# Sigmoid attention with a gated convolution: fewer groups in plain float32, and a new written-out order

## The chip, the cores and the metric

The kernel runs on one core of a Trainium2 chip. The metric is the device time of one execution in microseconds (us). The kernel before was run three times, with times of 561.61, 561.38 and 561.16 us (median 561.38).

## The reference

`q`, `k` and `v` have 8 batches, 12 heads, 448 positions and 64 columns per head, in float32. Cut to what matters, the reference computes:

```python
scores = q @ k.T / sqrt(64) - log(448)      # per batch and head
attn   = sigmoid(scores)                    # elementwise, no row sum
x      = heads_side_by_side(attn @ v)       # [8, 448, 768]
gate   = sigmoid(causal_conv(x, conv_w))    # 5 taps, per column
val    = x @ w_val                          # [768, 768]
out    = (gate * val) @ w_out               # [768, 768]
```

## The kernel before, in words

**Work units.** The 96 heads are 48 pairs (two heads lie on the 128 partitions), and two pairs are a group, so there are 24 groups. Three groups make one batch position block b of 448 + 64 columns on which the convolution and the two products by `w_val` and `w_out` run.

**Scores.** A pair's scores are three chunks of a PSUM tile `ps_a` (three buffers, taken in turn). If the pair is in `WHOLE_SCORES`, the operands are `qk_single` as loaded, in float32, and TensorE makes one pass in plain float32 (L575). Otherwise `split_qk` first makes `qk_hi` (a cast, L395 or L391) and `qk_lo` (a subtraction on GpSimd, L404), and TensorE makes three passes on these. In the trace, one plain float32 matmul is two instructions.

**Attention.** If a group is in `WHOLE`, ScalarE writes the sigmoid of a tile into `a_single` (L611), and TensorE multiplies that by `v_src` as loaded (L661 for the 64 positions left over, L669 for the chunks). Otherwise there is more to do for the group. VectorE takes the largest value of each row of `v_src` (`vm`, L590); TensorE sums it over partitions with a small matmul (L595) that shares the tile and the step with the left-over scores (L598), so these scores wait for `vm`; VectorE makes the exponent `v_exp` from the sum (L603, L632, L634, L636); `v_src` is split in `v_hi` and `v_lo`; and each sigmoid tile is written in place into `ps_a` (L611), scaled to float16 by ScalarE (L399) and its remainder taken by VectorE (L622).

**After the attention.** The result is copied out of `ps_a` into `x` (L391, L395, or L399 with a scale). VectorE takes `x_max` (L717). A small matmul with `diagonal` (L761) spreads the largest value of a block, and `x` is split into `xs` (L804). The five taps of the convolution make `gate`: a first scaling, then for each tap either a multiply-and-add by VectorE (L738), or a scaling into `tap` and a DMA that adds `tap` to `gate` (L742, a gate sum). L744 is the gate's sigmoid.

**Weights.** Twelve blocks of `w_val` and `w_out` come as 64-bit words. `convert` and `weight` turn each into float32 with five steps (L425, L427, L401 or L399, L450, and the largest value, L453). For each two blocks TensorE sums the largest values over partitions (L463), VectorE makes the scales (L435, L437, L439), and the blocks are split into `w_hi` and `w_lo` (L401 or L399, then L490).

**What sets the order.** Nothing is scheduled on the chip or in the build: every operation gets a number when the program is laid out, and the table `ORDER` (two characters for an operation) says in what order they are issued, `ENGINES` (one letter each) on which engine each runs. Within an engine the instructions run in that order, and loads stand in it too, on SyncE's queue (SP). GpSimd's instructions take turns with VectorE's on a shared port. `v_src` has two buffers, so the load of a group waits until the attention two groups before it has ended.

Of the kernel before, what the change touches and what calls it, by code (L numbers as in the profile page):

```python
# [37 lines left out]
WHOLE = {0, 1, 2, 3, 4, 5, 6, 7}  # L38
WHOLE_SCORES = {0, 1, 2, 3, 4, 5, 6, 7, 8, 9, 10, 11, 12, 13, 14, 15}
# [70 lines left out]
    "0d3x4009423D4443453E4s3F3G3H3J4t3K4u4y484d3L0b494v463M4w4a4O4b3W4x4C4c4A0c4D4F4E4e4G4f4I0g4H4B4J4g0e1c4L1d4K4h"  # L110
    "4M574i584P4j5d594k4l4Q4N4m4q4o5a5b4R4p4n4U5c5h5f5i5k4r5j5l4S5w5n5m5Y5o0j5q5g5p0h5r4V0f5R6J4W0k5S4T5T5X4X5s4Y5U"
    "5x5V5y4Z5W5z4+5+7u7v6e5Z6K4-500i51606f536h52556g6i546k6j5A6l5C6n96976m5t610m6o676C6862566D6p6E5-6q6I0n636F646G"
    "5B656H5D6-3I5E6L70726N5F715G7375745H76786677796O5I696r7n5J5K5L6s7o5P7p5u5N7a5O6P7q6a6Q6w7t0l7r6R9U6b6M7s7M6S7w"
    "6c5v7N5Q7P7O7x7Q7S0p7R6x0o7T7b7y7V6t7U7Y6u7W8-6U7Z90be6V6y7+95916vbf7X7-80929V6z81826A93836T7z94846W7A9p0r987B"
    "9q856X7C9r6d868i1e8999878j8a9s7D8b6Y9t888k9u8l6Z7E9b8c7c7F8m6B7G8d9cca8e7d7H8n8fbg9v8g9w9y5M9z9x9A9a9E9C8o8r1g"
    "0q9G8s9D9H8A7I8B9d7h1faX8t9F7Je98C7ebh8u9f7f7K8D6+9J8E1h9g8Fbi8p8vbj9I9e8w9Kbk8x8G9M8y0s9h9L1i7i9N9R7g1k9S9Obl"
    "abbm9P1jacbn9i9T7L1l9Qbo9jag0u9W8hbpfmahaj0tai7jam8J1mak8z8K9l8L9Z9X9m8H8S7k8Tal8Man9k9Bad8q8U1nbq8Nap9Y7l8Oaq"
    "8V7mbrae8Waoea8X1o9+asaraY8Iat8Pauav8Y1pcfaJ8Qcg9naDawaxco8RaG1qchaf8ZciaEcp9-cja1ayaMbscqa28+craHfna0csazaFct"
# [1146 lines left out]
```

## Time and profile before

| | before |
|---|---|
| median of three runs (561.16 to 561.61) | 561.38 us |
| span of the profiled execution | 559.5 us |
| TensorE (PE) busy | 554.8 us (99%) |
| VectorE (DVE) busy | 487.4 us (87%) |
| ScalarE (ACT) busy | 429.7 us (77%) |
| GpSimd (POOL) busy | 200.8 us (36%) |

The span goes from the first instruction to the end of the last one in one profiled execution; the time of a run is some 1.9 us longer, by the median and the span. A busy TensorE isn't a TensorE at its peak, since the ends of matmuls are modelled; how long TensorE takes for a piece of work is read here from the start of one group of matmuls to the start of the next.

### The profile page before, as it was taken

Reading aid. Unit: us, or ns where it says so; the run is one execution under the profiler, and the core shown is the slowest. Engines: PE = TensorE matmul, PEld = TensorE weight load, DVE = VectorE, ACT = ScalarE, POOL = GpSimd, SP = SyncE. Lnnn points to the kernel's source line nnn. Section 1 sums busy time; section 2 is a strip of 40 time slices with the busy share of each in tenths; the row PEclk is TensorE's granted clock in tenths of the full one; section 3 lists DMA queues with packets and bytes.
Section 4 is the critical chain, followed back from the end, with each engine's and each line's share of the span. In section 5 each row is a group of like instructions: output and inputs, shape, how many; then the busy total and the mean of one; then the engine's idle time right before and its main releaser. Section 6 shows DMA issues by size and latency. Waiting matters only on the chain.

```text
span 559.5 us, 10606 instructions
## 1 busy us (share of the span) xinstructions
PE 554.8 (99%) x4061; PEld 325.1 (58%) x4061; DVE 487.4 (87%) x844; ACT 429.7 (77%) x572; POOL 200.8 (36%) x211
## 2 busy tenths in 40 slices
PE   9999999999999999999999999999999999999997
PEld 4343334455554567855466754678555874456686
DVE  1878999999999999998999999998899888896653
ACT  5676687889999989999989878899858978443220
POOL 0000012454345655535364653454523523404100
PEclk9999999999999999999999999999999999999999
DMA  8888687855776537576376685467365657437314
GB/s 294 298 306 282 202 264 145 206 129 130 176 188 148 133 97 199 110 208 136 74 177 169 148 175 147 128 150 190 94 158 127 158 100 169 77 76 134 74 36 154
DMA packets 40371, 89.04 MB, mean 159 GB/s; under 512 B 14976, under 2 KB 21248, under 8 KB 40320
## 3 DMA queue, kind: packets, MB, share of 16 engines
q1 hardware_dynamic: 30272, 55.58, 30.6%
q0 software_dynamic: 8928, 31.99, 30.2%
q10 hardware_dynamic: 1120, 0.79, 0.4%
q8 instruction: 32, 0.52, 0.4%
q14 instruction: 19, 0.16, 0.1%
HBM read 43.96 MB, written 12.40 MB: 101 GB/s over the span
## 4 chain that ended last, share of the span: by engine, by line
PE 99%; ACT 0%; DVE 0%; issue 0%
PE ps_m L1053 34%; PE ps_a L575 19%; PE ps_a L669 17%; PE ps_m L978 15%; PE ps_a L978 7%; PE ps_a L598 4%; PE ps_a L661 3%; PE ps_m L1096 1%; PE ps_m L463 0%; ACT y_mixed L399 0%; PE ps_a L764 0%; DVE ones L1089 0%; PE ps_m L761 0%; PE ps_a L463 0%; PE ps_a L595 0%
## 5 line engine op out<-in xcount | busy, mean ns | idle before, releaser
L1053 PE MATMUL ps_m<-xs,w_val_hi 128*128 128x512 f16 x504 | 150.1, 379 | 0.0
L611 ACT ACTIVATE ps_a<-ps_a 128x896 f32<-128x896 f32 x112 | 99.5, 907 | 16.5 <-PE ps_a L575 9.8
L742 POOL DMA_DIRECT2D gate<-tap x60 | 53.5, 892 | 152.9 <-DVE gate L738 37.3
L622 DVE SCALAR_TENSOR_TENSOR a<-ps_a,a 128x896 f16<-128x896 f32 x96 | 101.9, 1082 | 3.6 <-ACT a L399 3.5
L1053 PE MATMUL ps_m<-xs,w_val_lo 128*128 128x512 f16 x252 | 95.5, 379 | 0.0
L404 POOL TENSOR_TENSOR qk_lo<-qk_src,qk_hi 128x448 fp32r<-128x448 f32 (+1 forms) x64 | 72.2, 1133 | 63.3 <-DVE qk_hi L395 11.5
L399 ACT ACTIVATE a<-ps_a 128x896 f16<-128x896 f32 x96 | 86.7, 921 | 0.6
L1053 PEld LDWEIGHTS <-w_val_hi 128*128 128x128 f16 x504 | 47.8, 98 | 56.0 <-issue 6.4
L978 PEld LDWEIGHTS <-mixed 128*128 128x128 f16 x648 | 62.4, 98 | 13.0 <-issue 3.7
L611 ACT ACTIVATE a_single<-ps_a 128x896 f32<-128x896 f32 x56 | 47.5, 925 | 11.1 <-PE ps_a L575 6.3
L978 PE MATMUL ps_m<-form,mixed 128*128 128x256 f16 x432 | 54.2, 273 | 0.0
L669 PE MATMUL ps_a<-a,v_hi 128*64 128x448 f16 x384 | 52.7, 354 | 0.0
L399 ACT ACTIVATE tap<-x,cw 128x512 f32<-128x512 f32 x62 | 44.4, 729 | 2.2 <-DVE x L720 2.2
L1053 PEld LDWEIGHTS <-w_val_lo 128*128 128x128 f16 x252 | 24.7, 98 | 29.7
L575 PE MATMUL ps_a<-qk_single 64*128 64x448 f32 x192 | 39.6, 558 | 0.0
L575 PE MATMUL ps_a<-qk_hi 64*128 64x448 f32 x192 | 39.5, 407 | 0.0
L669 PE MATMUL ps_a<-a_single,v_src 128*64 128x448 f32 x192 | 37.8, 543 | 0.0
L978 PE MATMUL ps_m<-form,w_out_hi 128*128 128x256 f16 x216 | 37.6, 273 | 0.0
L738 DVE SCALAR_TENSOR_TENSOR gate<-x,cw,gate 128x512 f32<-128x512 f32 x48 | 36.3, 760 | 0.1
L978 PEld LDWEIGHTS <-w_out_hi 128*128 128x128 f16 x324 | 31.2, 98 | 8.6 <-issue 1.8
L575 PE MATMUL ps_a<-qk_lo,qk_hi 64*128 64x448 f32 x192 | 35.4, 362 | 0.0
L575 PE MATMUL ps_a<-qk_hi,qk_lo 64*128 64x448 f32 x192 | 35.3, 361 | 0.0
(176 smaller groups left out, 1063.5 us busy)
## 6 DMA issues: line engine op xcount, KB each, us to landing
gate<-tap POOLq DMA_DIRECT2D x60, 512.0 KB, 5.1
qk_src<-qk SPq DMA_DIRECT2D x32, 448.0 KB, 4.1
v_src<-vs SPq DMA_DIRECT2D x24, 448.0 KB, 4.7
...
qk_single<-qk SPq DMA_DIRECT2D x15, 448.0 KB, 7.2
...
```

The source lines that it names most:

```text
L399: nc.scalar.activation(to, x, AF.Copy, scale=by)
L404: engines[eng].tensor_tensor(to, x, y, op=ALU.subtract)
L575: mm(b()[:, h, :S], k()[rows, at : at + P], q()[rows, :S], start=(n == 0), stop=(n == len(terms(i)) - 1))
L598: mm(b()[to, h, :S], x[n]()[rows, CW:], x[n]()[rows, :S], start=True, stop=True)
L611: nc.scalar.activation(to, b()[:, :, :S], AF.Sigmoid, bias=-math.log(S), scale=1.0 / math.sqrt(D))
L622: op({"V": 1.0}, t + 0.5, lambda e: nc.vector.scalar_tensor_tensor(part(1), p(), A_SCALE, part(0), op0=ALU.mult, op1=ALU.subtract), [b], [ ...
L661: mm(px()[to, p, :S], v()[rows, h * D : (h + 1) * D], x(s["a"])[rows, h, at : at + S], start=(j > 0 and n == 0), stop=(j == 0 and n == len ...
L669: mm(px()[to, p, :S], v()[:, o : o + D], x(st[2 * j + p]["a", c])[:, h, at : at + S], start=(j == 0 and c == 0 and n == 0), stop=(j > 0 an ...
L738: op({"V": 0.67}, at + AT["tap_step"] * k + AT["tap_pair"] * p, lambda e, p=p, part=part, k=k: nc.vector.scalar_tensor_tensor(part(), x()[ ...
L742: op({"G": 0.95}, at + AT["tap_step"] * k, lambda e, tap=tap: nc.gpsimd.dma_start(g(), tap(), accum_op=ALU.add), [tap], [g], 4 * P * T * 4 ...
L978: mm(to(), stat[a](), src()[:, f, :], start=(first and c == 0 and j == 0), stop=(c == NQ - 1 and j == 2), skip_group_check=True)
L1053: mm(po()[:, cs], w()[:, c, :], x(k)[:, cs], start=(c == 0 and j == 0), stop=(c == NC - 1 and j == 2))
```

## The change

Group 7 leaves `WHOLE`, and pairs 12 to 15 leave `WHOLE_SCORES`: their attention and scores are then made as those of the later groups are. `ORDER` and `ENGINES` are replaced as a whole, since the operations and their numbers change.

```diff
-WHOLE = {0, 1, 2, 3, 4, 5, 6, 7}
-WHOLE_SCORES = {0, 1, 2, 3, 4, 5, 6, 7, 8, 9, 10, 11, 12, 13, 14, 15}
+WHOLE = {0, 1, 2, 3, 4, 5, 6}
+WHOLE_SCORES = {0, 1, 2, 3, 4, 5, 6, 7, 8, 9, 10, 11}
...
 ORDER = (
-    "3U004z5e0102030504193s3y3e3f3h3g3i3k3j3l3n3m3o3q3p3N0a3r0608073O473P3t3u3Q1a3v3R3z3S1b3A3V3X3T3B3Y3w3+3Z3C3-41"
...
+    "48003u013v3w023x3A3y3z3D3B043C3E03053F3I3J3K3L3M063O07084n3N3P3Q3R3G0a414243443H0b45464b494c474d3S4e4f4h4i4g4k"
```

The two tables have two more lines in the change, so its line numbers are two higher: L592 in the rows of the change is L590 of before.

The first place is VectorE's beginning: the first two blocks of `w_val` up to the scales. Before:

```order
L425 TENSOR_SCALAR w_words<-w_words 128x768
L427 TENSOR_SCALAR w_words<-w_words 128x768
L425 TENSOR_SCALAR cw_words<-cw_words 128x30
L401 TENSOR_SCALAR w_words<-w_words 128x768
L425 TENSOR_SCALAR w_words<-w_words 128x768
L427 TENSOR_SCALAR cw_words<-cw_words 128x30
L427 TENSOR_SCALAR w_words<-w_words 128x768
L401 TENSOR_SCALAR w_words<-w_words 128x768
L450 SCALAR_TENSOR_TENSOR w_words<-w_words 128x768 x2
L453 TENSOR_REDUCE val_max<-w_words 128x1 x2
```

and in the change:

```order
L427 TENSOR_SCALAR w_words<-w_words 128x768
L429 TENSOR_SCALAR w_words<-w_words 128x768
L403 TENSOR_SCALAR w_words<-w_words 128x768
L452 SCALAR_TENSOR_TENSOR w_words<-w_words 128x768
L455 TENSOR_REDUCE val_max<-w_words 128x1
L427 TENSOR_SCALAR w_words<-w_words 128x768
L429 TENSOR_SCALAR w_words<-w_words 128x768
L403 TENSOR_SCALAR w_words<-w_words 128x768
L452 SCALAR_TENSOR_TENSOR w_words<-w_words 128x768
L455 TENSOR_REDUCE val_max<-w_words 128x1
```

Where steps of two blocks alternated, each block now goes through its five steps one behind the other, each step reading what the one ahead of it wrote. The same holds for the blocks that follow.

The second place is TensorE where the left-over scores of group 7 stand, behind the scores of pairs 12 and 13 (`diagonal` is the spread of the first block's largest value). Before:

```order
L575 MATMUL ps_a<-qk_single 128x448 x12
L598 MATMUL ps_a<-qk_single 64x448 x4
L661 MATMUL ps_a<-a_single,v_src 64x448 x4
L761 LDWEIGHTS ones
L761 MATMUL ps_m_757<-diagonal,ones 128x128
L669 MATMUL ps_a<-a_single,v_src 64x448 x12
L575 MATMUL ps_a<-qk_single 128x448 x6
```

and in the change, from the last chunk of pair 13:

```order
L577 MATMUL ps_a<-qk_hi 128x448 x2
L577 MATMUL ps_a<-qk_hi,qk_lo 128x448 x2
L577 MATMUL ps_a<-qk_lo,qk_hi 128x448 x2
L763 LDWEIGHTS ones
L763 MATMUL ps_m_771<-diagonal,ones 128x128
L597 LDWEIGHTS ones
L597 MATMUL ps_a<-vm,ones 128x1
L600 MATMUL ps_a<-qk_src 64x448 x4
L663 MATMUL ps_a<-a_single,v_src 64x448 x4
L671 MATMUL ps_a<-a_single,v_src 64x448 x12
```

The sum of `vm` now stands ahead of the left-over scores, and the small matmul of `diagonal` has moved ahead of both.

The third place is VectorE just ahead of that `vm`. Before, around the `x_exp` that makes `diagonal`:

```order
L717 TENSOR_REDUCE x_max<-x 128x2
L425 TENSOR_SCALAR w_words<-w_words 128x768
L720 COPY x<-x 128x2x6x4
L401 TENSOR_SCALAR w_words<-w_words 128x768
L755 TENSOR_REDUCE x_exp<-x_max 128x1
L450 SCALAR_TENSOR_TENSOR w_words<-w_words 128x768
L401 TENSOR_SCALAR tap<-x,cw 128x512
```

and in the change:

```order
L452 SCALAR_TENSOR_TENSOR w_words<-w_words 128x768
L455 TENSOR_REDUCE out_max<-w_words 128x1
L505 TENSOR_SCALAR y_scale<-val_inverse,y_inverse 128x6
L397 CAST qk_hi<-qk_src 128x448
L397 CAST qk_hi<-qk_src 128x384
L437 TENSOR_SCALAR out_inverse<-ps_m_728 128x2
L719 TENSOR_REDUCE x_max<-x 128x2
L757 TENSOR_REDUCE x_exp<-x_max 128x1
L592 TENSOR_REDUCE vm<-v_src 128x1
```

Casts of `qk_src` and the `vm` of group 7 stand here now, and the third block of `w_out` is converted ahead of them.

## Rows read from the trace of the kernel before

**Rows 1.** The page: the chain that ended last, share of the span by engine.

```profile
PE 99%; ACT 0%; DVE 0%; issue 0%
```

**Rows 2.** Busy time by engine in two stretches: PE, PEld, DVE, ACT, POOL, clock.

```profile
12.50:420.00 407.50, 407.50 (x2957) 226.86 (x2954) 383.43 (x659) 350.35 (x465) 164.64 (x168) 1.00 0.65 172
145.00:300.00 155.00, 155.00 (x1227) 93.23 (x1227) 149.50 (x258) 148.22 (x199) 80.64 (x81) 1.00 0.59 143
```

**Rows 3.** Timeline of PE, pairs 12 to 14: start, duration, engine, line.

```profile
72.94 4.78 PE L575 MATMUL ps_a<-qk_single 64*128 64x448 f32 x24
77.65 0.98 PE L598 MATMUL ps_a<-qk_single 64*64 64x448 f32 x8
78.45 0.93 PE L661 MATMUL ps_a<-a_single,v_src 64*64 64x448 f32 x8
79.32 0.23 PE L761 MATMUL ps_m<-diagonal,ones 128*128 128x128 bf16 x1
79.48 4.73 PE L669 MATMUL ps_a<-a_single,v_src 128*64 128x448 f32 x24
84.14 2.53 PE L575 MATMUL ps_a<-qk_single 64*128 64x448 f32 x12
86.60 0.60 PE L1053 MATMUL ps_m<-xs,w_val_hi 128*128 128x512 f16 x2
```

**Rows 4.** Timeline of PE, a group whose operands are split.

```profile
155.94 0.17 PE L595 MATMUL ps_a<-vm,ones 128*128 128x1 bf16 x1
156.04 0.98 PE L598 MATMUL ps_a<-qk_src 64*64 64x448 f32 x8
156.84 0.56 PE L661 MATMUL ps_a<-a_rest,v_hi 64*64 64x448 f16 x8
...
161.04 0.47 PE L575 MATMUL ps_a<-qk_hi 64*128 64x448 f32 x2
...
163.09 0.61 PE L1053 MATMUL ps_m<-xs,w_val_hi 128*128 128x512 f16 x2
```

**Rows 5.** Timeline of PE: the first two sums of the weights' largest values.

```profile
21.74 0.25 PE L463 MATMUL ps_m<-val_max,ones 128*128 128x1 bf16 x4
...
34.62 0.25 PE L463 MATMUL ps_m<-val_max,ones 128*128 128x1 bf16 x4
```

**Rows 6.** Timeline of DVE: in brackets the idle time ahead, and its releaser.

```profile
12.52 0.56 DVE L425 TENSOR_SCALAR w_words<-w_words 128x768 int32<-128x768 uint32 x1 [11.51 <-DMA w_words<-w_val]
...
22.03 0.16 DVE L435 TENSOR_SCALAR val_inverse<-ps_m 128x2 int32<-128x2 int32 x1 [1.62 <-PE ps_m L463]
...
42.84 0.56 DVE L425 TENSOR_SCALAR w_words<-w_words 128x768 int32<-128x768 uint32 x1 [0.36 <-DMA w_words<-w_val]
43.43 1.04 DVE L427 TENSOR_SCALAR w_words<-w_words 128x768 int16<-128x768 int16 x1
44.25 0.93 DVE L453 TENSOR_REDUCE val_max<-w_words 128x1 bf16<-128x768 f32 x1
45.09 0.55 DVE L401 TENSOR_SCALAR w_words<-w_words 128x768 f32<-128x768 f32 x1
...
62.78 0.19 DVE L720 COPY x<-x 128x48 f32<-128x48 f32 x1 [0.38 <-ACT x L391]
```

**Rows 7.** DVE's groups by line and shape: count, busy us, mean ns.

```profile
L622 DVE SCALAR_TENSOR_TENSOR a<-ps_a,a 128x896 f16<-128x896 f32 x96 | 101.9, 1082 | 3.6 <-ACT a L399 3.5
L738 DVE SCALAR_TENSOR_TENSOR gate<-x,cw,gate 128x512 f32<-128x512 f32 x48 | 36.3, 760 | 0.1
...
L590 DVE TENSOR_REDUCE vm<-v_src 128x1 bf16<-128x896 f32 x16 | 17.3, 1078 | 0.0
L427 DVE TENSOR_SCALAR w_words<-w_words 128x768 int16<-128x768 int16 x12 | 12.6, 1052 | 0.2
...
```

**Rows 8.** DMA issues: count, KB each, median us from issue to landing.

```profile
v_src<-vs SPq DMA_DIRECT2D x24, 448.0 KB, 4.7
```

**Rows 9.** ACT's largest group of scalings: count, busy us, mean ns.

```profile
L399 ACT ACTIVATE tap<-x,cw 128x512 f32<-128x512 f32 x62 | 44.4, 729 | 2.2 <-DVE x L720 2.2
```

More of the change, by code (lines that the diff above doesn't have):

```diff
@@ L108 @@
 ORDER = (
-    "3U004z5e0102030504193s3y3e3f3h3g3i3k3j3l3n3m3o3q3p3N0a3r0608073O473P3t3u3Q1a3v3R3z3S1b3A3V3X3T3B3Y3w3+3Z3C3-41"
[L110 to L118, printed above, removed]
@@ new lines @@
+    "094l4j4m4I4J3T3U3V3W3X3Z3+4P4K4L4M4N4S3-4O4T4Q4V4U4W4X5u4t404o4p4q0d4r4s4u52194Y4Z4-504+5n5o4v0c4w4x5p5q4y4a4z"
+    "4A5t4B0e5r1a4C4D4E4F4G1b4H5354515s5v5x5y5A5z5B5D5C5G5E5F5H5I65666768696a55564R57585M1c0g0h6c6d595a5b5c5d5e6b6e"
+    "5N5O5f0f6u5g5h6x0j6v5j1d6w6A6y6f6B6z6D6E6C5k6S6T6U6V5w1e6W6g5S5P5l6F6n6X6Y6o6h1g6q6i6j6k0k6Z7K0i1f6-7f7g1h7h7i"
+    "7l7j7m7k7o7n7D7p7E6+5J5m9qat6G6l6m5Q5T6p7q5R71725U5V780l7F7G7H735W74751i3Y1k1j1l5i5K5X707I7J806r6H0m0n796I766J"
+    "0o6s777M7a8182837L6K6L5L5Y1m1o1n8486878589885Z7N8c8d8e9f8a1p9g9i9j7P8b9k9l1q8f5+8g0p7Q8h5-619h9n629J8i636t9m8j"
@@ new lines @@
+    "9o8l7O7b9O9r1s9s8k9p649K9L8m6M9P8n9R9Q0r6N9S8y8z6O8A8p6P8o8q8r8s8t8u8B1u8C1r9U6Q9V9X1tbw1wbP9Y9T1v9M9v7V8D6R7r"
+    "9W8v9Z8EbQ9+7W7c0qaia11xbRau7R9N7S7T7U9-a07d8w8Fa9aca28H9u7s8Q8I8R8S8J8T8U8V8K8Gaaada31y1z9wa5afa7ab1Aae7taga8"
+    "8La68M7X1Baj7e7u7xbSakalaqarahbTbUeK0s8N8O7Yamanaoapas8Wav8XbVaRaSaTaM8P7ZaN7v7w0ufX8Z8+96aO97987y7z7A7BaXaU7+"
+    "a+bW9zaVaYa-bX999a7CaW1C1DaZbY8Yb07-8x8-9b90919293b1b2b4bZ1E9cb3b51Fb+60a494bc0tbd9dbl9e959xbe9yaP9C9A9BbfaQcQ"
+    "cRcLbicZb-c+c-cSd0cTcUd1cVd2b6c0bgbhbjbk1Gbac1b7bm0v0xc2bncK9Db89Ebtboc5c6c7bubpcMc3cWbqaxbraybscabyc4b9bvbx1I"
@@ new lines @@
+    "cb9td3f11Hawccd6df1Jf2d4bzd50wcmdgdhcd1K1LazezcXaA9Fcecnd7dicgch9Gf3cjckcff4aBciclaCd8d9djaDda9HdkeLf5dbaEc8bb"
+    "codcbBdlcpcYcrc9f6cqcydocvcwczdpdqcBaFf7f8f91MdxdydzfacscAdA1NdBdCcxbCdrfbaGaIcCds1O1Qdt0A1PeA1RcDfMeBfjfkbAeC"
+    "fceDeEeFeG9IfdduaHfeeHeIdDffflctcucEcGeJeMcFfofpcHfucIfqfrde0yaJfsdGdNdOcJbDcNfmfgfv0z1Sft1UdmbFfxdd1Tdwdnfwfy"
+    "bEdHdIfzdPdQdJaKh81VfhePdKeQfibGdRdSgedLfAbHfBfCdMfDdZfGfEfHfJfKdTfndUe4e5d+d-gfe0dVggeOfFfNfI0DfPfObIbJghfQfU"
+    "fVdWfRfLeNaLfW0BdXfSfTgBbKgih9cOfZgZeRgEgFgC1WgDe1gj1Xe2bLbM1+1Y1Z0CgkeSglgmgwgxe3gygGe6e7e820gHe9eagKegbNehgI"
@@ L182 @@
[L182 to L185 removed]
+    "GSPSPPSAPAAAPSPASSASVVVVSSSSSVVVVPSPPPPASPPPAPAPVAAPPAASAPAPPVPVVVVVGPPPPPAAPAAPAAGSVVVVSVVVSSPPAAPPPVSVVPPVSP"
@@ L186 @@
+    "PPVAAAPPVAPPPPPVVVVSVPPPVPPVVSPPPAGSVGPPAAAVAVVVVPVVAVVPPPPAPVVVVPGPPAGPPVAAVVAPVVPVPSPAAAPAPVPAPPPVPPGAAGPVVV"
+    "PVAVVVAAPVAPPVVPPPVVAVPVVVVVPPPAASSSPAPPPAVVPPVPPGAPAPAVVGAPPAVAVPPVVVPVPVPPPPGPAPPVVPPVAAPPPGAAPVVVVVVPPPGVPA"
+    "PPPPPPPPVVVPPGPPPAPPAPPPVPVAPPPVPPAVPAGVPPSPPVAPPPPPAVVVPPGVVVSPPASSGAPPPPPAVVGPPPPVPPPPPVAPVVPPAPPVPPVASPPPPV"
+    "PPAPVPPAPPVPSPAPSPPPPPPVPPASVPPPVSPPPVSPPPPAPPAPPPAVPPPVPPPPAPPPPVPPPVPPPPPVPPSPSSVSAAVAPPVPSPSPPPPVSPASSPPPPA"
+    "PAAS"
 )
```

120 lines of the change are left out of this document (55 added, 65 removed).

## The prediction, made before the change was run

> **What bounds the kernel now.** I read the chain that ended last first: TensorE holds 99% of it [rows 1]. The busy time by stretch then says that this isn't an average over stages: from 12.5 to 420 us TensorE is busy for 407.5 of 407.5 us, and for 155.0 of 155.0 between 145 and 300 [rows 2]. So nothing that only the other engines save can shorten this kernel. Time comes from shorter matmul work alone, and it is lost as soon as TensorE has to wait. The same rows show how near the others are: between 145 and 300 us VectorE is busy for 149.5 and ScalarE for 148.2 of 155 us. TensorE's granted clock is 1.00 in both stretches, its upper level, so I leave the clock out of the sum.
>
> **The change on TensorE.** Prices are from the start of one piece to the start of the next. The plain scores of two pairs cost 77.65 - 72.94 = 4.71 us, and those of a pair with a product behind it 86.60 - 84.14 = 2.46 [rows 3]. A split pair's cost 163.09 - 161.04 = 2.05 [rows 4]. Pairs 12 to 15 go from 4.71 + 2.46 + 2.46 = 9.63 to 4 x 2.05 = 8.20, a saving of 1.43. A plain group's attention costs 79.32 - 78.45 for the left-over positions and 84.14 - 79.48 for the chunks, 0.87 + 4.66 = 5.53 [rows 3]; a split one's is 161.04 - 156.84 = 4.20, and the sum of `vm` adds 156.04 - 155.94 = 0.10 [rows 4]. Group 7 saves 1.23. The rest of TensorE's instructions are the same in number and shape. **The floor is 2.66 us lower**: 556.9 us of span if TensorE never waits.
>
> **What the new table makes TensorE wait for.** Group 7's left-over scores now stand behind the sum of `vm`. TensorE is there early: it begins pair 12 at 72.94 as before (the pieces ahead are the same ones), then come two split pairs and one sum of 0.18 (79.48 less 79.32 is 0.16 for the like), so 72.94 + 4.10 + 0.18 = 77.2. Behind the wait everything of TensorE is queued, so each microsecond there is a microsecond of the run, unless TensorE would have waited later anyway.
>
> VectorE's arrival is a sum over its order. From the first weight block, which lands at 12.52 [rows 6], it has 96 instructions up to and with that `vm`. By the means of their forms they last 62.9 us: nine conversions of a block (0.56, 1.05, 0.96 and 0.95 each, seven of them with a scaling of 0.56 as well) 35.6, eight multiply-and-adds of 0.760 6.1, `vm` 1.08, and 43 others 20.1 [rows 6, 7]. Starts decide what such a sum becomes. At 43.43 an instruction that needs the result of the one ahead starts 0.03 us behind its end, and at 45.09 one that doesn't starts 0.09 before the end [rows 6]. Of the 96, 41 are of the first kind (short chains were rarer before: 28 of the first 150, now 46) and 55 of the second, which I set at 0.08: 62.9 + 1.2 - 4.4 = 59.7.
>
> To that come waits. The first sum of largest values stood at 21.74 on TensorE [rows 5]; the table puts a piece of left-over scores (0.80) and one of left-over attention (0.87) ahead of it, so 23.4, and VectorE read the result 0.29 later [rows 5, 6]: 23.7, where the ten conversion steps are done at about 21.0. That is 2.7. The second sum stood at 34.62 [rows 5]; half of a group's chunks (2.33) is now ahead of it, so it is read at 37.2, and VectorE is there at 35.1: 2.1. The third keeps its place and meets no wait. Late copies by ScalarE cost VectorE 0.38 at 62.78 [rows 6]; I put 0.5 for such. The sum is 12.5 + 59.7 + 2.7 + 2.1 + 0.5 = 77.5 for `vm`'s end.
>
> The other bound on `vm` is its data. `v_src` has two buffers, so group 7's load is issued after group 5's attention, that is, at 72.94 when pair 12 begins. The median landing of 4.7 us [rows 8] gives 77.6, and 1.08 for `vm` 78.7. TensorE, which makes the sum of `diagonal` in between (0.16), thus waits from 77.4 to between 77.6 and 78.8. **I take 1.0 us**, nearer the load, since a maximum of the two decides; the bounds are 0 and 2.0 (a late load).
>
> **The stretch behind it.** From that `vm` up to the second chunk of pair 16, TensorE has 0.1 + 0.8 + 0.87 + 4.66 of group 6 and 7, two pairs of 2.05, two products of 7.8 (84.14 to 86.60 was the pair ahead of the first), sums, and group 8's `vm`, left-over scores, split attention and one chunk: 32.1 us. VectorE has 53 instructions in the same stretch, since the chunk needs a `ps_a` buffer that VectorE's remainder of group 8 (L622, 1.08 each [rows 7]) frees: 36.4 us by their means, five chained, so 36.4 + 0.2 - 3.8 = 32.8. TensorE waits 0.7 there, if VectorE has no other wait. The chunk after it needs the buffer that ScalarE's copy of group 7's result frees, another 0.2 or so. **0.9**, bounds 0 and 1.8.
>
> **ScalarE later.** By the order, ScalarE's durations sum to 20.0 us more than before (18 more `tap` scalings of 0.729 alone are 13.1 [rows 9]), VectorE's to 2.5 less. Some 6 us lie in group 7 before 125 us, and about 4.3 between the pieces of TensorE that stood at 145 and 300. There ScalarE was idle for 155 - 148.2 = 6.8 us [rows 2], and 2.5 would be left. If its idle time can be filled so far, this costs nothing; if none of it can, 4.3. Gaps of an engine that others feed don't close wholly: **0.6**. GpSimd gets 24 more gate sums, and was busy for 80.6 of those 155 us: nothing, and 0.5 at most. The 24 multiply-and-adds that VectorE loses for them bring nothing by themselves, since TensorE never waited for VectorE there.
>
> **Sum.** 559.53 - 2.66 + 1.0 + 0.9 + 0.6 = 559.4 of span. The median of the runs is 561.38 against a span of 559.53, so 1.85 lies around it: **561.2 us**, a no change by what a measurement of this kernel can tell (0.2%, or 1.1 us).
>
> **A rule against this sum.** The rows at 43.43 and 45.09 [rows 6] price a dependence at 0.12 us, which is 4.9 us for 41. The Trainium skill, page "VectorE: DVE Perf Modes", section "The DRAIN you can't avoid", states that eight copies with a semaphore after each last as long as eight with one at the end: "the semaphore costs nothing extra here". By it the chains would be free. This case's trace doesn't agree where steps are chained; what the rule would make of the time is rival 1.
>
> **Rivals.**
> 1. *No waits: the floor.* If the chained steps cost no more than others, VectorE is 4.9 us earlier, at 72.6, and only the load decides: landed within 3.2 us of 72.94, it lets `vm` end by 77.2 and TensorE meets it ready. The stretch behind starts with VectorE ahead, and its 0.7 is gone too. Then 558.7, up to 560.2 with one of the smaller waits left. For it: sums of means err by 1 us easily over 65 us, and the waits are of that size. Against it: two independent sums (order and load) put `vm` behind TensorE.
> 2. *Slower: ScalarE is full.* If ScalarE's 6.8 us of idle time between 145 and 300 are waits that remain, its 4.3 us push TensorE back by as much: 558.7 + 1.9 + 4.3 = 564.9 with the waits ahead; half of it gives 562.8. It decides from 1.9 us on above the floor and the early waits, that is, if over 4.4 of ScalarE's 6.8 us stay. For it: ScalarE and VectorE are both over 95% busy there [rows 2], and each feeds the other. Against it: the extra scalings have no successor on TensorE for long.
> 3. *The waits merge.* If the load of group 7 is 2 us late, the stretch behind has that slack and its own wait vanishes: -2.66 + 2.0 + 0.6, again 561.3.
>
> **How the numbers follow.** The forecast (with rival 3), 560.3 to 562.5: 0.41. Rival 1, 558.7 to 560.2: 0.33. Rival 2, 562.5 to 565: 0.26. Faster by over 0.2% is rival 1, slower is rival 2. The likeliest case's own range is 560.3 to 562.5; the range that leaves out 2 in 10 runs from 558.9, just above the floor, to 563.6.
>
> **What the changed profile would show.** The floor: twelve pairs of plain scores, and TensorE's time from first to last matmul, less its idle time, 2.7 us shorter. The wait: TensorE idle about 1 us between 77 and 79, put down to VectorE's `vm`, and VectorE reading the first two sums at about 23.7 and 37.2 after 2 to 3 us of idle time. The stretch: TensorE idle before a chunk of pair 16's scores near 110. ScalarE: busy for over 151 of the 155 us that answer to 145 to 300, and no idle time of TensorE there. I am wrong if TensorE shows no idle time up to 120 us (rival 1), or over 2 us after it (rival 2).

## The result, and the profile after

The changed kernel took 565.63 us (median of four runs, 565.06 to 566.88), the kernel before 561.5 beside it: a ratio of 1.008, 95% interval 1.0067 to 1.0092. It is 4.1 us slower, beyond the slow end of the stated range (563.6). The profiled execution is the longest of the four, 566.88 us with a span of 565.1; one part of it, pointed out below, is in no other of the four by their mean clocks (0.996 here, 0.999 to 1.0 there).

The page of the changed kernel, the lines that answer to the table of before and to [rows 1], and the row of the granted clock in 40 slices:

```profile
span 565.1 us, 10771 instructions
PE 555.5 (98%) x4102; PEld 327.5 (58%) x4102; DVE 489.4 (87%) x819; ACT 448.5 (79%) x606; POOL 221.8 (39%) x239
PEclk9999989999999999999999999999999999999999
PE 72%; DVE 16%; ACT 4%; DMA 3%; issue 3%; POOL 1%; SPq 0%; DVEq 0%; POOLq 0%; ACTq 0%
```

TensorE had the last word in 99% of the span [rows 1] and now has it in 72%: the chain leaves it for VectorE, for ScalarE and for transfers. The shares of busy time hardly moved, and would not have told this. The waits of TensorE say where, with total us, number and longest:

```profile
PE ps_m L1055 <- DVE v_exp L638: 1.5, 1, 1.5
PE ps_m L1098 <- DVE ones L1091: 1.1, 1, 1.1
PE ps_a L597 <- DVE vm L592: 0.9, 1, 0.9
PE ps_a L577 <- ACT x L393: 0.6, 1, 0.6
PE ps_m L763 <- ACT diagonal L401: 0.5, 1, 0.5
PE ps_m L980 <- DVE y L403: 0.5, 1, 0.5
PE ps_a L577 <- DVE a_rest L624: 0.5, 1, 0.5
PE ps_a L577 <- ACT x L401: 0.2, 1, 0.2
```

The second row is ahead of the first matmul, as before; the others are new (one of 0.2 at 6.88 us, for a load, is left out). Four of them lie between 72 and 114 us, where the prediction looked for waits; the longest, at 190, and the one at 212 lie where it had put 0.6 us in all. In the timeline of TensorE, the first stretch (it answers to [rows 3]) and the two later places:

```profile
72.46 0.47 PE L577 MATMUL ps_a<-qk_hi 64*128 64x448 f32 x2
...
74.49 0.47 PE L577 MATMUL ps_a<-qk_hi 64*128 64x448 f32 x2 [0.55 <-ACT x L393]
...
77.23 0.36 PE L577 MATMUL ps_a<-qk_hi,qk_lo 64*128 64x448 f32 x2
77.44 0.36 PE L577 MATMUL ps_a<-qk_lo,qk_hi 64*128 64x448 f32 x2
78.32 0.22 PE L763 MATMUL ps_m<-diagonal,ones 128*128 128x128 bf16 x1 [0.52 <-ACT diagonal L401]
79.41 0.18 PE L597 MATMUL ps_a<-vm,ones 128*128 128x1 bf16 x1 [0.87 <-DVE vm L592]
79.51 1.77 PE L600 MATMUL ps_a<-qk_src 64*64 64x448 f32 x8
81.06 1.72 PE L663 MATMUL ps_a<-a_single,v_src 64*64 64x448 f32 x8
82.71 4.83 PE L671 MATMUL ps_a<-a_single,v_src 128*64 128x448 f32 x24
87.47 0.47 PE L577 MATMUL ps_a<-qk_hi 64*128 64x448 f32 x2
...
89.50 0.61 PE L1055 MATMUL ps_m<-xs,w_val_hi 128*128 128x512 f16 x2
...
113.68 0.47 PE L577 MATMUL ps_a<-qk_hi 64*128 64x448 f32 x2 [0.46 <-DVE a_rest L624]
...
165.68 0.60 PE L1055 MATMUL ps_m<-xs,w_val_hi 128*128 128x512 f16 x2
...
192.16 0.59 PE L1055 MATMUL ps_m<-xs,w_val_hi 128*128 128x512 f16 x2 [1.48 <-DVE v_exp L638]
...
212.33 1.14 PE L980 MATMUL ps_m<-form,mixed 128*128 128x256 f16 x9 [0.49 <-DVE y L403]
```

From pair 12 to the product behind pair 14 TensorE takes 89.50 - 72.46 = 17.04 us; by the prices of [rows 3, 4], three split pairs, two small sums more and the rest of group 6 are 12.9. Of the 4.1 too much, 1.94 is idle time in three rows. Another 1.53 is no wait: the left-over scores last 81.06 - 79.51 = 1.55 us and the left-over attention 82.71 - 81.06 = 1.65, where [rows 3] have 0.80 and 0.87. The stretch has this clock (columns: us, busy time of PE, PEld, DVE, ACT, POOL, then the clock):

```profile
79.60:82.70 3.10, 3.10 (x16) 0.71 (x16) 2.61 (x12) 2.56 (x5) 0.00 (x0) 0.50 0.26 65
```

0.50 is the lower of the two levels, 1.2 GHz; TensorE had been idle for 1.39 of the two microseconds ahead. By its mean clock this is the part that the other three runs don't have. The rest, 0.6, is not idle time in the trace (PE is busy for 7.65 of the 9.60 us from 70 to 79.6, and the three waits make up the rest). It comes from how a wait is counted. Running matmuls overlap: those at 77.23 and 77.44 start 0.2 apart and last 0.36. A wait is counted from the end of the last one, so by the starts each wait costs about 0.16 more than its row says.

The product that stood at 163.09 [rows 4] is a mark that every version has. Here it starts at 165.68, 2.6 us later than before, though the 2.66 us of matmul work that the change saves all lie ahead of it. The other 3.0 of the 5.6 us by which the span grew are lost after it, where the work is the same.

This mark can't be compared by itself from profile to profile, because the first pair's scores take a different time in each. TensorE's first left-over scores start at 9.79 in the profile of before, at 9.33 here, and anywhere from 8.70 to 9.98 in the others, and what is won or lost there is carried along (the change's profile is 0.46 ahead there and still 0.45 ahead at 28 us). From these scores to the product it is 165.68 - 9.33 = 156.35 us here and 163.09 - 9.79 = 153.30 before: 3.05 longer, 1.5 of it the lower clock.

VectorE at 78 us, with the load that it waits for, and at 190 us (idle time in brackets), then GpSimd at 188 us:

```profile
77.67 0.16 DVE L757 TENSOR_REDUCE x_exp<-x_max 128x1 f32<-128x6 f32 x1
78.26 1.09 DVE L592 TENSOR_REDUCE vm<-v_src 128x1 bf16<-128x896 f32 x1 [0.43 <-DMA v_src<-vs]
...
188.62 1.29 DVE L403 TENSOR_SCALAR mixed<-mix 128x384 f16<-128x384 f32 x1
189.94 1.24 DVE L877 SCALAR_TENSOR_TENSOR mixed<-mix,mixed 128x384 f16<-128x384 f32 x1
...
191.36 0.75 DVE L1065 SCALAR_TENSOR_TENSOR gate<-ps_m,y_scale,gate 128x512 f32<-128x512 f32 x1
192.03 0.14 DVE L638 TENSOR_SCALAR v_exp<-v_exp 128x1 f32<-128x1 f32 x1
```

```profile
72.57 0.33 SPq L536 DMA_DIRECT2D v_src<-vs  x1
```

```profile
188.05 2.71 POOL L406 TENSOR_TENSOR qk_lo<-qk_src,qk_hi 128x448 fp32r<-128x448 f32 x2 [2.69 <-DVE mix L867]
```

At 78 the data came last: the load was issued at 72.57 and VectorE could start `vm` 5.7 us later, though it had been done with its own work at 77.83. At 190 two VectorE instructions on `mixed` lasted 1.29 and 1.24 us beside two of GpSimd's subtractions, and TensorE waited for the read of PSUM behind them. The profile names the last `v_exp` step (L638) as what ended that wait, but the product doesn't read `v_exp`. The bank that it needs is, by the code and the times, the one that the gate product (L1065) reads; that read ended at 192.11, and TensorE started at 192.16.

### The profile page after: what moved, and what is told of

The parts are those of the page before. It is cut to its first block, busy times and chain, and to the rows that moved or that the text cites. A ratio compares the mean times of both kernels' runs of the same rounds, so it can differ in the third digit from the quotient of the medians.

```text
span 565.1 us, 10771 instructions
## 1 busy us (share of the span) xinstructions
PE 555.5 (98%) x4102; PEld 327.5 (58%) x4102; DVE 489.4 (87%) x819; ACT 448.5 (79%) x606; POOL 221.8 (39%) x239
## 4 chain that ended last, share of the span: by engine, by line
PE 72%; DVE 16%; ACT 4%; DMA 3%; issue 3%; POOL 1%; SPq 0%; DVEq 0%; POOLq 0%; ACTq 0%
PE ps_m L1055 22%; PE ps_m L980 14%; PE ps_a L577 13%; PE ps_a L671 12%; PE ps_a L980 7%; DVE a L624 3%; PE ps_a L600 3%; PE ps_a L663 2%; ACT ps_a L613 1%; DVE gate L740 1%; DMA gate<-tap 1%; DMA v_src<-vs 1%; DVE gate L1065 1%; DVE a_rest L624 1%; DVE form L406 1%
## 5 line engine op out<-in xcount | busy, mean ns | idle before, releaser
L406 POOL TENSOR_TENSOR qk_lo<-qk_src,qk_hi 128x448 fp32r<-128x448 f32 (+1 forms) x72 | 81.1, 1134 | 153.9 <-ACT qk_hi L393 58.6
L613 ACT ACTIVATE ps_a<-ps_a 128x896 f32<-128x896 f32 x119 | 106.0, 905 | 17.5 <-PE ps_a L577 11.8
L624 DVE SCALAR_TENSOR_TENSOR a<-ps_a,a 128x896 f16<-128x896 f32 x102 | 107.9, 1083 | 3.1 <-ACT a L401 2.9
L401 ACT ACTIVATE a<-ps_a 128x896 f16<-128x896 f32 x102 | 91.0, 918 | 1.4
L401 ACT ACTIVATE tap<-x,cw 128x512 f32<-128x512 f32 x80 | 55.7, 723 | 7.9 <-DMA gate<-tap 7.9
L577 PE MATMUL ps_a<-qk_hi 64*128 64x448 f32 x216 | 44.5, 408 | 1.3 <-ACT x L393 0.6
L613 ACT ACTIVATE a_single<-ps_a 128x896 f32<-128x896 f32 x49 | 41.3, 927 | 5.4 <-PE ps_a L577 3.3
L577 PE MATMUL ps_a<-qk_lo,qk_hi 64*128 64x448 f32 x216 | 39.6, 362 | 0.0
L671 PE MATMUL ps_a<-a,v_lo 128*64 128x448 f16 x204 | 36.3, 352 | 0.0
L671 PE MATMUL ps_a<-a_single,v_src 128*64 128x448 f32 x168 | 33.4, 545 | 0.0
```

The costliest lines, as they stand in the source:

```text
L401: nc.scalar.activation(to, x, AF.Copy, scale=by)
L406: engines[eng].tensor_tensor(to, x, y, op=ALU.subtract)
L577: mm(b()[:, h, :S], k()[rows, at : at + P], q()[rows, :S], start=(n == 0), stop=(n == len(terms(i)) - 1))
L613: nc.scalar.activation(to, b()[:, :, :S], AF.Sigmoid, bias=-math.log(S), scale=1.0 / math.sqrt(D))
L624: op({"V": 1.0}, t + 0.5, lambda e: nc.vector.scalar_tensor_tensor(part(1), p(), A_SCALE, part(0), op0=ALU.mult, op1=ALU.subtract), [b], [ ...
L671: mm(px()[to, p, :S], v()[:, o : o + D], x(st[2 * j + p]["a", c])[:, h, at : at + S], start=(j == 0 and c == 0 and n == 0), stop=(j > 0 an ...
```

## The experiments

All runs are compared with the kernel before on the same chip (medians there 561.16 to 561.57). In the kernels with moved operations `"a behind b"` issues operation a directly behind b, and nothing else changes. In e2 to e4, e8, e9 and e11 this is a list beside the table; in e10 and e12 to e15 the moves are written into the table itself. What the two-character names are is said each time; they are those of the change's table. For the runs that carry the argument, the medians and ratios stand here together with rows of the profiled execution: the start of the first left-over scores, the start of the product that stood at 163.09, the time between the two, and the time from the product to the end of the span.

| run | median us | ratio to before | scores at | product at | between | behind |
|---|---|---|---|---|---|---|
| before | 561.38 | | 9.79 | 163.09 | 153.30 | 396.4 |
| after | 565.63 | 1.0080 (1.0067 to 1.0092) | 9.33 | 165.68 | 156.35 | 399.4 |
| e6: new order, both sets as before | 564.70 | 1.0067 (1.0054 to 1.0080) | 9.43 | 163.09 | 153.66 | 400.5 |
| e5: new order, group 7 plain | 563.98 | 1.0053 (1.0039 to 1.0068) | 8.70 | 162.09 | 153.39 | 398.9 |
| e4: after, the two `mixed` moved | 564.44 | 1.0064 (1.0047 to 1.0080) | 9.73 | 164.27 | 154.54 | 398.0 |
| e11: after, GpSimd's work moved | 564.06 | 1.0049 (1.0037 to 1.0062) | 9.04 | 163.80 | 154.76 | 398.3 |
| e14: e5, GpSimd's work moved, copy early | 563.71 | 1.0038 (1.0027 to 1.0050) | 9.64 | 163.22 | 153.58 | 397.9 |
| e15: e6, GpSimd's work moved | 563.98 | 1.0050 (1.0038 to 1.0062) | 9.87 | 163.43 | 153.56 | 398.8 |

Where the intervals of two versions overlap, as they mostly do below the first two rows, it is not clear which of the two is faster.

### Is the lower clock a cost of its own?

The first kernel (e1) keeps TensorE at work where it waits:

```diff
+            for _ in range(8 if j == 7 else 0):
+                mm(b()[:, 1, :P], ones(), ones(), start=True, stop=True)
...
+            for _ in range(5 if b == 1 else 0):
+                mm(to[:, :P], ones(), ones(), start=True, stop=True)
```

The eight stand ahead of the sum of `vm`, the five ahead of the matmul of `diagonal`; they add work and change no value.

> The change, with 5 small matmuls of ones added ahead of the small matmul of diagonal and 8 ahead of group 7's sum of vm, so that TensorE has work while it waits there (their results are overwritten). Both theories expect the granted clock to stay at its upper level between 79 and 83 us, group 7's left-over scores and left-over attention at 0.80 and 0.87 us (1.55 and 1.65 in the change), and pair 14's scores to begin near 86.0 instead of 87.47. Theory A (the lost clock is a term of its own, on the path): the time falls by 1.6 us. Theory B (VectorE's order sets when pair 16's second chunk can begin, at 113.7, whatever TensorE did before): TensorE's wait near 113 grows from 0.6 to about 2, and the time falls by 0.5 us or less. I hold B for the likelier.

It measured 566.35 us, ratio 1.0096 (1.0080 to 1.0113). Its profile, from its longest run, shows TensorE behind the added matmuls:

```profile
78.29 0.61 PE L597 MATMUL ps_a<-ones 128*128 128x128 bf16 x8
81.22 0.16 PE L599 MATMUL ps_a<-vm,ones 128*128 128x1 bf16 x1 [2.33 <-DVE vm L592]
81.32 0.98 PE L602 MATMUL ps_a<-qk_src 64*64 64x448 f32 x8
82.12 0.93 PE L665 MATMUL ps_a<-a_single,v_src 64*64 64x448 f32 x8
```

The left-over scores take 0.80 us again, the upper clock's price, even behind a wait of 2.33 us; `v_src` came later still in this run. The run gained nothing, and neither theory's sign came: no fall of 1.6 us, and a wait of 0.65 at 114 where theory B had about 2. With the later `v_src` it is no clean test of the clock. That the clock isn't the 4 us is shown by the change itself: its three runs without the lower clock took 565.06 to 566.15.

The times of the single runs say more. A mean clock of 0.996 or 0.997 marks a run in which it fell. In each of the five kernels that have runs with and without the fall, those with it took longer: 1.8 us in the change, 1.1 to 1.6 in e8, e9 and e13, and 2.9 in e4. Whether the clock costs this, or longer waits make both, these runs don't separate.

### Can `vm` come earlier?

Five moves (e2): the loads of pairs 14 and 15 (0m, 0n) behind group 7's `v_src` load (0o), and the `x_max`, `x_exp` and `vm` (7N, 8c, 9f) ahead of the rest of VectorE's work there.

```diff
+MOVED = ("0m behind 0o", "0n behind 0m", "7N behind 6K", "8c behind 7N", "9f behind 8c")
```

> The change, with five entries of the order moved: the loads of pairs 14 and 15 behind group 7's load of v_src, and on VectorE x_max, x_exp and vm ahead of a largest value, a scale and two casts. Expected by both: v_src lands by 77, vm is done near 77.5, TensorE waits for less than 0.3 us at the small matmul of diagonal and at vm together (1.4 in the change), and the clock doesn't fall. Theory A (each wait is a term of its own): the time falls by 1.4 + 1.6 = 3.0 us. Theory B (VectorE is late for pair 16's chunk anyway): the wait near 113 grows to about 2.5 us and the time falls by 0.9 to 1.4 us. A third outcome, no change, would say that both waits only mirror a full VectorE.

It measured 568.92 us, 1.0136 (1.0121 to 1.0150), with the lower clock in all four runs. VectorE is early, and waits:

```profile
79.18 1.09 DVE L610 TENSOR_REDUCE vm<-v_src 128x1 bf16<-128x896 f32 x1 [2.72 <-DMA v_src<-vs]
```

TensorE waits 1.70 us for `vm`, and 0.91 us at 81 for a `qk` load that had been put back. So the load sets this wait, not VectorE's order. The next kernel (e8) took that away: group 7's `v` in a buffer of another pool, which is free early, so that its load stands at 62.46 instead of 72.57 (with the `x` copy and `vm` early as well).

```diff
-        v = two[j]["v"] = v_src.new()
+        v = two[j]["v"] = v_src.new() if j != 7 else form_ring.new(
+            lambda: sb.tile([P, VW], F32, name="v_form", tag="form", bufs=FORMS))
...
+MOVED = ("0o behind 0l", "6J behind 7M", "7N behind 7M", "8c behind 7N", "9f behind 8c")
```

> The change with group 7's v_src in a buffer of its own (one of those of form, which nothing uses so early), its load moved ahead in the queue, ScalarE's copy of group 5's result ahead of a scaling, and x_max, x_exp and vm ahead of the conversion behind them on VectorE. Both theories: the load lands before 72 us, vm is done by 76.5, and TensorE has no wait over 0.2 us between 73 and 80 (0.6, 0.5 and 0.9 in the change); the clock stays up. Theory A (these waits are terms of their own): the time falls by 2 to 2.6 us, to 563 to 563.6. Theory B (VectorE and ScalarE are too full up to 113): the wait near 113 grows to about 2 us and the time falls by under 0.8 us.

567.22 us, 1.0108 (1.0091 to 1.0125): no wait for `vm` in the profile, but ScalarE was held up by a gate sum, and its copy of `x` came late:

```profile
72.04 0.74 ACT L419 ACTIVATE tap<-x,cw 128x512 f32<-128x512 f32 x1 [3.98 <-DMA gate<-tap]
```

The early load and the gate sums lie close together there (that one slows the other is not shown); TensorE waits 1.14 and 0.55 us for `ps_a` buffers instead, and its clock falls behind these (0.50 from 77.4 to 80.7). The wait for `vm` is real, and taking it away brought no gain.

### The waits at 113 and at 190, by VectorE's order

One kernel (e3) puts two splits of `w_out`, a load and two scalings (a6, a8, 7x, bS, 7u) behind the reads that group 8's chunk waits for (ah, ar), as at 113 us VectorE read the `vm` sum only at 110.46, behind two of those splits. Another (e4) puts the two `mixed` instructions (gl, gm) behind the gate product and the last `v_exp` step (gy) near 190.

```diff
+MOVED = ("a6 behind ah", "a8 behind a6", "7x behind a8", "bS behind 7x", "7u behind ar")
...
+MOVED = ("gl behind gy", "gm behind gl")
```

> The change, with two splits of w_out, the load and the scaling behind them moved behind group 8's v_exp on VectorE, and one scaling on ScalarE moved behind group 8's a_rest. In the change VectorE reads group 8's sum of vm 2.3 us after TensorE made it, since two splits of 1.0 us stand ahead. Theory A (an order that puts the urgent instruction late): the wait of 0.6 us at 113 goes, and the time falls by 0.5 to 1.0 us. Theory B (VectorE as a whole is full): the wait comes back within 30 us at the next chunk or product, and the time stays within 0.3 us.

> The change, with two instructions on the mixed weights (1.29 and 1.24 us in the trace, 0.36 and 0.55 by their medians, stretched while GpSimd runs two subtractions) moved behind VectorE's gate product and v_exp near 190. Theory A: TensorE's wait of 1.5 us for a PSUM bank at 190.7 goes, and the time falls by about 1.5 us. Theory B (VectorE is full, and what is late here is late at the next bank): the wait of 0.5 us at 212 grows by about as much, and the time falls by under 0.5 us.

The first measured 565.47 us, 1.0072 (1.0060 to 1.0084), as after and as theory B had it: the wait at 113 became waits of 0.39, 0.30 and 0.49 us between 111 and 139. The second measured 564.44, 1.0064 (1.0047 to 1.0080): the wait at 190 is gone, all that came back is one of 0.23 at 194, and the median is 1.2 us lower, though the intervals overlap. All these moves together with the own buffer, and a copy of `y` ahead at 209 (e9):

```diff
+MOVED = ("0o behind 0l", "6J behind 7M", "7N behind 7M", "8c behind 7N", "9f behind 8c",
+         "a6 behind ah", "a8 behind a6", "7x behind a8", "bS behind 7x", "7u behind ar",
+         "gl behind gy", "gm behind gl", "cP behind ia", "g0 behind cP")
```

> The own buffer and its moves, the early v_exp of group 8, the two mixed weights behind the gate product at 190, and at 212 the copy out of the PSUM bank ahead of a scaling. Theory A: the gains add, 2.3 + 0.5 + 1.2 + 0.5, so 561 to 561.8, about the kernel before. Theory B (what is taken from one wait comes back at the next): 563 or more.

567.27 us, 1.0109 (1.0089 to 1.0130), like the one with the own buffer: waits of 1.14 and 0.55 at 75 and 77 us, 0.87 at 114, and at 216 one of 1.17 for a copy that the moved one had put back.

### Which part of the change costs it

The new order with group 7 plain (e5: only the first set goes back, so only the scores' half of the change of sets is left), and with both sets as before (e6); operations that these don't have are left out of the table, and nothing else is moved but one load of e6 (of pair 17, a little later; no wait of that profile is for it).

```diff
-WHOLE = {0, 1, 2, 3, 4, 5, 6}
+WHOLE = {0, 1, 2, 3, 4, 5, 6, 7}
...
-WHOLE_SCORES = {0, 1, 2, 3, 4, 5, 6, 7, 8, 9, 10, 11}
+WHOLE_SCORES = {0, 1, 2, 3, 4, 5, 6, 7, 8, 9, 10, 11, 12, 13, 14, 15}
```

> The change with group 7 back in WHOLE: its 21 operations of splitting leave the table, the rest keeps its order and engines. TensorE's matmul work is 1.2 us longer than in the change. Theory L (the wait at vm is the load of v_src, which is issued only when group 5's attention ends, and the waits up to 140 come from VectorE's extra work for group 7): TensorE waits for at most 0.3 us behind the small matmul of diagonal, the wait near 113 is gone, and the time is 563.4 to 564.6, 1 to 2 us below the change. Rival T (the waits come from the new order as a whole, whichever group is split): they stay, and the time is 566.5 to 567.

> Both sets as before the change, with the change's order and engines (37 operations leave it, the rest keeps its place; one load stands a little later). TensorE's matmul work is that of the kernel before. Theory L: what is left of the loss is in the order alone, above all the 1.5 us at 190 and 0.5 to 0.9 at 212, so 563 to 564.2. Rival S (the loss is all in the split of group 7 and pairs 12 to 15): 561.4, as before. Rival T (the order costs all): 566 or more.

Group 7 plain: 563.98, 1.0053 (1.0039 to 1.0068). This is in theory L's range, and the waits behind the matmul of `diagonal` and at 113 are gone, as it said. Both sets as before: 564.70, 1.0067 (1.0054 to 1.0080), between theory L (up to 564.2) and rival T (566 or more), and far from rival S. This is the run that the verdict rests on, so its waits and its product are shown, and below them the first left-over scores of before and of e5:

```profile
PE ps_m L1053 <- DVE v_exp L636: 1.5, 1, 1.5
...
PE ps_a L575 <- DVE v_exp L632: 0.7, 1, 0.7
PE ps_m L978 <- DVE y L401: 0.5, 1, 0.5
...
PE ps_m L978 <- DVE form L404: 0.2, 1, 0.2
```

```profile
163.09 0.61 PE L1053 MATMUL ps_m<-xs,w_val_hi 128*128 128x512 f16 x2
```

```profile
9.79 0.98 PE L598 MATMUL ps_a<-qk_single 64*64 64x448 f32 x8
```

```profile
8.70 0.98 PE L598 MATMUL ps_a<-qk_single 64*64 64x448 f32 x8
```

With the work of before, the new table (its order and its engines) takes 153.66 us from the left-over scores to the product, 0.4 more than before, and loses 4.1 us of span behind it. Of these 2.9 are in rows of waits, at 188, at 208 and 209, and at 290 us, all for VectorE; the rest is in part the overlap lost at each wait. The profile is from the longest of the five runs. **The new table alone costs 564.70 - 561.16 = 3.5 us.**

The changed sets on top add 0.7 us by the ratios, which is within the noise. The profiles show why they bring nothing: what they save is eaten ahead of the product. The scores' half (e5) has 1.43 us less matmul work than e6, and its stretch up to the product is only 0.3 shorter: TensorE waits 0.46 and 0.51 us at 73 and 77 for ScalarE, which e6 doesn't, so these waits come with the split pairs and not with the table. (That e5 reaches the product at 162.09 is its early start, at 8.70.) With group 7's half too, in e11, where the clock doesn't fall, the stretch is 1.4 longer than in e5, for 1.23 less matmul work.

A kernel between the two (e13), with two of the four pairs split, was meant to show whether ScalarE (0.90 us for a chunk's sigmoid) is outrun by four split pairs in a row:

```diff
-WHOLE_SCORES = {0, 1, 2, 3, 4, 5, 6, 7, 8, 9, 10, 11, 12, 13, 14, 15}
+WHOLE_SCORES = {0, 1, 2, 3, 4, 5, 6, 7, 8, 9, 10, 11, 12, 13}
```

The diff is against the kernel before. The table is the change's without the operations that this kernel doesn't have, with gl and gm behind gy, cP and g0 behind ia (the first copy of `y` near 209), and the load of pair 15 later.

> Group 7 plain, and only pairs 14 and 15 split (each with a product behind it), the change's order, and the same two places mended. TensorE's matmul work is 0.8 us shorter than in the kernel before. Theory A (four split pairs in a row outrun ScalarE's sigmoids; two with products between don't): no wait between 70 and 145, so 0.8 us under the run with both sets as before and the same two moves, 561.3 to 562. Rival: the waits at 73 and 77 come with the order and stay, so no gain against it.

567.78, 1.0106 (1.0091 to 1.0122), with a wait of 2.21 us for `qk_src` at 79 us, for that load. So it says nothing on ScalarE.

### VectorE's order, or GpSimd beside it?

Five runs. First the sets of e5 with eight operations moved (e10): gl and gm behind gy, cP and g0 behind ia, and early on a weight's scaling on ScalarE (6J), `x_max` and `x_exp` (7N, 8c) behind ScalarE's copy of `x` (7M), and `diagonal` (8d) two sigmoids earlier. Then the sets of before with the first four of these (e12).

> Group 7 plain, pairs 12 to 15 split (as the run with group 7 plain, 564.0), and nine entries moved: the two mixed weights behind the gate product at 187, the copy out of PSUM ahead of a scaling at 208, ScalarE's copy of group 5's result ahead of a scaling at 72, x_max and x_exp ahead of a conversion, and diagonal two sigmoids earlier. Theory A (these waits are places where the order puts an urgent instruction late): the waits of 1.5 at 187, 0.5 at 208, 0.5 at 73 and 0.5 at 77 go, and the time is 561 to 561.8, about the kernel before. Theory B (they come back as others, since VectorE and ScalarE are full): 563 or more.

> Both sets as before the change with the change's order (564.7), and the mixed weights behind the gate product and the copy out of PSUM ahead of a scaling. Theory A: what the order alone costs (3.3 us) is mostly these two waits (1.65 and 0.95 us by their starts), so 562.1 to 562.8; the wait of 0.7 at 290 is left. Theory B: 564 or more.

They measured 564.27, 1.0046 (1.0033 to 1.0059), and 564.94, 1.0063 (1.0050 to 1.0075): no better than without the moves, as theory B had it. The wait at 188 is gone in both, and both have the same new one, 1.16 us at 211, for the next copy of `y`:

```profile
PE ps_m L978 <- DVE y L1001: 1.2, 1, 1.2
```

So the move at 209 cures a wait of 0.48 and brings one of 1.16: what was pushed behind the first copy of `y` makes the next one late. (e4, without that move, keeps 0.49 there and has no such wait.) Then the other way: VectorE's order stays, and the two subtractions of GpSimd (1Y, 1Z) and one load move behind the two `mixed` instructions, in the changed kernel (e11). The turns on the shared port are one-sided in the code: a GpSimd instruction is made to wait for the VectorE instruction ahead of it in the table (at 188.05 for `mix`, L867, which ended at 188.04), VectorE's next one isn't made to wait for GpSimd. So this move keeps the two apart:

```diff
+MOVED = ("1Y behind gm", "1Z behind 1Y", "0C behind 1Z")
```

> The change with VectorE's order untouched, and GpSimd's two subtractions (and one load) near 188 moved behind VectorE's two mixed weights. Theory P (the two instructions are stretched because GpSimd's subtractions run at the same time): they take about 0.36 and 0.55 us instead of 1.29 and 1.24, TensorE's wait at 190.7 shrinks from 1.5 to under 0.4 us, and the time falls by about 1.2 us, as it did with the two moved behind the gate product. Rival O (they are long for another reason): they stay at 1.2 to 1.3 us, the wait and the time stay.

564.06 us, 1.0049 (1.0037 to 1.0062). VectorE at that place:

```profile
186.78 0.35 DVE L419 TENSOR_SCALAR mixed<-mix 128x384 f16<-128x384 f32 x1
187.17 0.56 DVE L893 SCALAR_TENSOR_TENSOR mixed<-mix,mixed 128x384 f16<-128x384 f32 x1
```

0.35 and 0.56 us instead of 1.29 and 1.24: GpSimd's concurrent work had stretched them, and without it the wait at 190 is gone. The median is 1.6 us lower than that of the change, and the intervals don't overlap: theory P. In the kernel before, the same two stood 20 us earlier, with no subtraction beside them, and took 0.36 and 0.55. The last two runs apply this to e5 (e14), with the four early moves of e10 (6J, 7N, 8c, 8d), and to e6 (e15).

> Groups 0 to 7 and the scores of 12 pairs plain (so only the scores' half of the change of sets), after's order, with GpSimd's two qk_lo and the last load of that stretch behind the two mixed-weight instructions, and ScalarE's copy of x ahead of its scaling early on. Theory P+L (the waits that were found are separate and their mends add up): the run of these sets alone was 563.98; less 1.5 for the wait at 187 us and about 0.8 for the two waits of 0.46 and 0.51 near 73 and 77 us gives 561.7 (561.2 to 562.3), and no TensorE wait over 0.4 us between 180 and 195 us. Theory B (what is taken away in one place comes back in another): 563.5 to 564.3, with new waits over 1 us behind the mended places.

> Both sets as before, after's order, with GpSimd's two qk_lo and the last load of that stretch behind the two mixed-weight instructions. Theory P (GpSimd's work beside them stretches the two VectorE instructions, and this is the wait of 1.51 us at 188 us): 564.70 less 1.5 gives 563.2 (562.8 to 563.7), the two instructions take about 0.35 and 0.56 us. Theory B: 564.3 to 565, the wait comes back at 209 to 212 us. If theory P holds in both runs, the first is faster than the second by the scores' floor (1.4 us) or a little more.

563.71, 1.0038 (1.0027 to 1.0050), and 563.98, 1.0050 (1.0038 to 1.0062). Both waits at 188 are gone. The time of e14 lies in theory B's range, though without its new waits of over 1 us; that of e15 lies between its two theories. For the order alone, the distance to before falls from 3.5 to 2.4 us, by 1.1 of the 1.5 expected. For the scores it falls from 2.8 to 2.1 and not to the 0.5 or so that the mends would add up to. Up to the product e14 is no shorter than e5 (153.58 against 153.39): the waits at 75 and 77 are down to 0.41 and 0.22, and one of 0.33 came at 137. Behind the product e14 gains 1.0 and e15 1.7 in their profiles. The scores' saving shows as 0.3 us between the two medians, not 1.4, and that is within the noise. What is left of the table's cost in the second is largest at 206 to 210 us; TensorE there, and below it in the kernel before:

```profile
206.11 0.39 PE L978 MATMUL ps_m<-form,w_out_hi 128*128 128x256 f16 x2
...
208.20 0.38 PE L978 MATMUL ps_m<-form,mixed 128*128 128x256 f16 x2 [0.17 <-DVE form L404]
209.06 1.14 PE L978 MATMUL ps_m<-form,mixed 128*128 128x256 f16 x9 [0.48 <-DVE y L401]
210.04 0.38 PE L978 MATMUL ps_m<-form,w_out_hi 128*128 128x256 f16 x2
```

```profile
205.34 0.39 PE L978 MATMUL ps_m<-form,w_out_hi 128*128 128x256 f16 x2
...
206.34 2.13 PE L978 MATMUL ps_m<-form,mixed 128*128 128x256 f16 x18
208.30 0.38 PE L978 MATMUL ps_m<-form,w_out_hi 128*128 128x256 f16 x2
```

The same 27 matmuls up to the next `w_out_hi` take 210.04 - 206.11 = 3.93 us against 2.96, a loss of 0.97 for a `form` and a copy of `y` that VectorE makes late. Nothing is stretched here (the copy takes 0.48 us, and the subtraction of `form` 1.23, as before). It is the table: before, ScalarE makes all three copies of `y` at that place (206.75, 207.56, 208.77), and the new table gives one to VectorE (208.53), behind `form` and a scaling. No run takes this place away without a new wait, so its price is read from the trace alone. No version beat the kernel before.

## Why the prediction was wrong, point by point

**The bound, and the floor.** Right: TensorE's lost time is the run's lost time. A split pair costs 89.50 - 87.47 = 2.03 us, forecast 2.05. That the saving exists said nothing of the end: no run shows it at the product, since it is waited away ahead of it.

**The sum.** The span was to shrink by 0.2 us and grew by 5.6. From the first left-over scores to the product it was to shrink by 2.66 - 1.0 - 0.9 = 0.8 and grew by 3.05; the lower clock of this one run aside, that is 2.3 too much. Behind the product 0.6 was put and 3.0 measured, 2.4 too much. So two parts of the sum failed by about the same, and the second is the one that a wrong mechanism made.

**VectorE's order up to `vm`.** Near in its parts: VectorE read the first two weight sums at 23.24 and 36.86 us after 2.68 and 2.15 us of idle time; forecast 23.7 and 37.2 after 2.7 and 2.1. It was free for `vm` at 77.83, so `vm` would have ended at 78.9 by the order (forecast 77.5) and ended at 79.35 by the load (forecast 78.7). TensorE's wait was 0.52 for `diagonal` and 0.87 for `vm`, 1.4 against the 1.0, within 0 to 2.0, and the load set it, as the two runs that moved `vm` and the load showed (e2, e8).

**The stretch behind.** 0.46 at the chunk of pair 16 (113.68), and 0.63 in e4 and e11, where the clock didn't fall, against 0.9 with ScalarE's copy. Right in its place, and smaller; a wait for a copy of ScalarE came later (0.25 at 140).

**What was not priced between 72 and 90.** The wait of 0.55 at 74.49 for a `ps_a` buffer that ScalarE's late copy of `x` frees, the 0.16 or so by which each wait costs more than its row, and in this one run the lower clock (1.53). The forecast put waits of 1.0 and 0.9 in this part; with these terms it would have put 3 or more. The sentence that left the clock out of the sum rested on rows of a kernel that never waited; a forecast with waits had lost that ground.

**The step that failed: "ScalarE later: 0.6", with GpSimd at "nothing, and 0.5 at most".** Behind the product the loss is 3.0 us in the profile of the change, and 4.1 in that of the new table alone. The step asked whether ScalarE's added work fits its idle time, and put nothing for where the table places VectorE's and GpSimd's work. ScalarE didn't come out as forecast either: it was to be busy for over 151 of the 155 us and was for 147.0, so its idle time was not filled. But no wait of TensorE behind the product is for ScalarE. They are for VectorE. At 190 two instructions of 0.35 and 0.56 us, stretched by GpSimd to 1.29 and 1.24, stand ahead of a read of PSUM on which TensorE waits (1.48; gone in e4, e11, e14 and e15). At 209 to 212 a copy of `y` stands behind other work, with nothing stretched (0.49, and 0.97 with what goes with it). That such work stands close together could be read off the table, and a price for the stretch stood in the trace of before: a `mixed` scaling at 107.78, begun during a subtraction of GpSimd, took 0.81 us there and 0.35 or 0.36 elsewhere. The sum of an engine's durations over 155 us hides a wait of 1.5 us for one read of 0.75.

**The rivals.** The slower one named the side, but the wrong engine, and 565.63 lies above its 562.5 to 565. Its condition came true in the number (ScalarE idle for 8.0 of the 155 us, where it asked for over 4.4), but no wait of TensorE there is for ScalarE. The merging of waits was seen in part: mends before 145 us came back at other places (e3, e9). The floor, with 0.33, was never near: with the two buffers no run shows `v_src` landing in time, and where it did (e8) other waits took the place of this one.

**What stays open.** What the lower clock costs by itself: runs in which it fell took longer, but it also falls behind long waits. What the places at 209 and 290 us cost, beyond their rows: no run takes them away cleanly. Why the mends fall short of their sum in the medians, when single profiles can differ by a microsecond from the start on: in the kernel before, the first pair's matmuls last up to 1.11 us, in e5 up to 0.66, where the usual one takes 0.54, and the left-over scores start at 9.79 and 8.70. What decides that from run to run is not shown.
